# Top-k attention with a gated feed-forward layer: scores of two units ahead of the P@V of two others on TensorE

## The chip, the cores and the metric

The kernel runs on one core of one Trainium2 chip. A core has TensorE (matrix products, which write to PSUM), VectorE, ScalarE and GpSimd (elementwise work), and SyncE, whose queue issues most of the DMA transfers. Each engine runs its own instructions in the order in which they are written, and waits for the others through semaphores. The metric is the time of the whole program in device microseconds (us). Six runs of the kernel before took 1509.61 to 1519.95 us, median 1514.18.

## The reference

Attention over 8 batches of 8 heads, 576 positions, 64 elements a head, in which each query keeps only its 32 largest scores; then a feed-forward layer with g = h cos h.

```python
scores = scale * np.matmul(q, k.transpose(0, 1, 3, 2))          # (8, 8, 576, 576)
kth = np.partition(scores, -top_k, axis=-1)[..., -top_k:-top_k + 1]
scores = np.where(scores >= kth, scores, -1000000000.0)
attn = np.exp(scores - np.max(scores, axis=-1, keepdims=True))
attn = attn / (np.sum(attn, axis=-1, keepdims=True) + 1e-09)
attn_out = np.matmul(attn, v)
x = attn_out.transpose(0, 2, 1, 3).reshape(B * S, H * D)         # (4608, 512)
h = x @ w_in                                                     # w_in (512, 2048)
out = (h * np.cos(h)) @ w_out                                    # w_out (2048, 512)
```

All inputs are float32.

## The kernel before

**Units and slots.** The 4608 query rows are cut into 36 tiles of 128 rows, the 8 heads into 4 pairs. A unit is one tile of rows with one pair of heads: 144 units, in the order of the tiles. 576 is four and a half tiles, so that every ninth tile holds rows of two batches; its units have two parts, and their products are split into 64 rows each. The main loop (L778) takes one unit per slot. In slot i several units are worked on at once, each at another stage:

- u = unit i: VectorE looks for its 32nd largest scores. `topk_first` folds the 576 scores into 288 larger and 288 lesser ones (`fold`, L247, twice), reading the first half out of PSUM (`sc`) and the second out of the SBUF copy `s`; then come rounds of MAX8 and MATCH_REPLACE8 (L307, L310).
- w = unit i-1: ScalarE masks and exponentiates its scores (`bounds`, `mask`, `exponentials`, L312 to L342).
- x = unit i-2: VectorE takes the reciprocal of the sums (L346), GpSimd multiplies (L351) and splits the 32-bit words into halves (L363); SyncE's queue writes them to DRAM (`write_halves`, L368) and reads them back transposed (`transposes`, L374) into `pT`.
- z = units i-4 and i-3, in even slots only: TensorE forms P@V for both (`values`, L411, 20 matmuls a unit in program order, or 40 with two parts), and ScalarE copies the result to `xT` (`take_values`, L417).
- units i+1 and i+2, in even slots: TensorE forms their scores (`scores`, L223). By the condition at L609 the third unit of a tile with two batches is scored one slot ahead in place of two, so that the even slot before it scores one unit alone. ScalarE copies one unit's scores to `s` in each slot (`take_scores`: L233 for columns 0 to 447, L234 for the last 128).

The feed-forward layer is fed between these by `feed`, in portions: `ff1` (L468, 16 matmuls of 128x128) and `ff2` (L546, two of 128x512 in program order). The profile counts two matmul records for each float32 matmul. Copies of finished banks (L481, L556), the reduction of the angle on GpSimd (L507 to L516), the sine on ScalarE (L526) and the product on GpSimd (L533) follow.

**PSUM.** `sc` has two buffers of two banks; a unit's buffer is free when the second fold has read it, so the scores of unit i+2, formed in slot i, need the second fold of unit i in that same slot. One more tile of two banks, `rim`, holds three things: the last 128 score columns of two units (`sc_ends`), and, behind them, `room[0]`, in which P@V is built, and `room[1]`. The two banks of `mm` and `o` serve the feed-forward layer.

**Order.** The order on each engine is the order of the calls in the source; nothing reorders it. An even slot calls, for the parts that matter here: VectorE's search; `feed(1)`; `values(z)`; `scores` of units i+1 and i+2; on ScalarE `bounds` and `mask` of w, `exponentials`, `take_values(z)`, `take_scores(units[i + 1])`; then `load_weights`, `normalise`, `split`, `write_halves`, `transposes` of x, the loads of q, k and v that `at_slot` places in this slot (L188 to L204), `feed` again, twice. Slots 0 to 8 are `early_slot`, those after 140 `last_slot`; `slot` is used for 9 to 140. z is there from slot 12 on.

The buffers that bear on the order: q and k five, v six, `s` four, `pT` three, `xT` five.

Of the kernel before, what the change touches and what calls it, by code (L numbers as in the profile page):

```python
# [31 lines left out]
def kernel(  # L32
# [100 lines left out]
    def decode_second(n):  # L133

        for _ in range(min(n, len(wq["second"]))):
            st, w = wq["second"].popleft()
            wi = w.bitcast(I32)
            nc.vector.tensor_scalar(
                out=wi, in0=wi, scalar1=3, scalar2=None, op0=ALU.logical_shift_left
            )  # L140
            nc.vector.scalar_tensor_tensor(
                out=wi, in0=st[:, :, 1], scalar=-(2**31), in1=wi, op0=ALU.bitwise_and, op1=ALU.bitwise_or
            )
            wq["third"].append((st, w))
# [13 lines left out]
    units = []  # L158
# [57 lines left out]
    def scores(u):  # L216
        sc = u["sc"] = ps.tile([P, 2, 512], F32, tag="sc", name="sc", bufs=2)
        for to, k0, k1 in ((sc, 0, SB), (sc_ends[u["n"] % 2], SB, S)):
            for j in range(2):
                d = slice(j * D, (j + 1) * D)  # L220
                for b, q0, rows, r0 in u["parts"]:
                    st = pairs[b, u["hp"]]
                    nc.tensor.matmul(  # L223
                        to[r0 : r0 + rows, j, 0 : k1 - k0],
                        st["q"][d, q0 : q0 + rows],
                        st["k"][d, k0:k1],
                        start=True,
                        stop=True,
                    )

    def take_scores(u):
        s = u["s"] = work.tile([P, 2, S], F32, tag="s", name="s", bufs=4)
        nc.scalar.copy(out=s[:, :, 0:SB], in_=u["sc"][:, :, 0:SB])  # L233
        nc.scalar.copy(out=s[:, :, SB:S], in_=sc_ends[u["n"] % 2])  # L234
        if not u["folds"]:
            del u["sc"]
# [23 lines left out]
    def topk_first(u, w):  # L260

        u["top"] = tops[u["n"] % len(tops)]
        merges = [merge_first, merge_second] if w and w["folds"] else []
        if u["folds"]:
            for op in (ALU.max, ALU.min):
                fold(u, op)
                if merges:
                    merges.pop(0)(w)
        else:
            u["rest"] = work.tile([P, 2, S], F32, tag="rest", name="rest", bufs=1)  # L270
        for merge in merges:
            merge(w)
        topk_round(u, 0)

    def topk_round(u, rnd):
        top, rest, lasts = u["top"], u["rest"], TOPK // 8 - 1
        end = TOPK - 1 - 8 * rnd
        at = top[:, :, end : end - 8 if rnd < lasts else None : -1, 0]
        if u["folds"]:
            search(at, rest[:, :, 0:HS], rest[:, :, 0:HS], rnd < lasts)  # L280
            if rnd < TOPK // 16:

                low = top[:, :, 1 + 8 * rnd : 9 + 8 * rnd, 1]
                search(low, rest[:, :, HS:S], rest[:, :, HS:S], rnd < TOPK // 16 - 1)
        else:
            search(at, u["s"] if rnd == 0 else rest, rest, rnd < lasts)
        if rnd == lasts:
            del u["rest"]
# [44 lines left out]
    def exponentials(u):  # L333
        s, nd = u["s"], u.pop("nd")
        den = u["den"] = small.tile([P, 2], F32, tag="den", name="den")
        for j in range(2):
            nc.scalar.activation(  # L337
                out=s[:, j], in_=s[:, j], func=AF.Exp, bias=nd[:, j : j + 1], scale=1.0,
                accum_out=den[:, j : j + 1],
            )  # L340

        nc.scalar.activation(out=den, in_=den, func=AF.Identity, bias=eps, scale=1.0)  # L342

    def reciprocal(u):
        u["rden"] = small.tile([P, 2], F32, tag="rden", name="rden")
        nc.vector.reciprocal(u["rden"], u.pop("den"))  # L346
# [106 lines left out]
    def ff1(blk, i):  # L453
        w = blk["w"]
        nf = 256 // w
        part = i % 4
        if part == 0:
            blk["g"].append(ffw.tile([P, 1024], F32, tag="g", name="g", bufs=CHUNKS))
            ff["live"] += 1
        if part % 2 == 0:  # L460
            open_bank()
            blk["mm"] = ps.tile([P, 512], F32, tag="mm", name="mm", bufs=2)
        g, mm = blk["g"][-1], blk["mm"]
        for a in range(nf):
            f = i * nf + a
            at = (part % 2 * nf + a) * w
            for c in range(NC):
                nc.tensor.matmul(  # L468
                    mm[:, at : at + w],
                    w_in[f // FC][:, c, (f % FC) * P : (f % FC + 1) * P],  # L470
                    blk["xT"][:, c],
                    start=c == 0,
                    stop=c == NC - 1,
                )
        if part % 2 == 0:
            return
        ff["open"] -= 1
        full.append((take_first, blk, g, mm, part // 2))
# [6 lines left out]
    def take_banks():  # L485
        while full:
            take, *what = full.popleft()
            take(*what)
# [30 lines left out]
    def sines(least):  # L519

        n = sum(c[3] < ff["now"] for c in waiting)
        if n == 0 or (n < least and waiting[0][3] + 2 > ff["now"]):
            return
        for _ in range(n):
            blk, g, x, _, scale = waiting.popleft()
            nc.scalar.activation(out=x, in_=x, func=AF.Sin, bias=halfpi, scale=scale)  # L526
            sined.append((blk, g, x))
# [8 lines left out]
    def ff2(blk, i, f0):  # L536
        w = blk["w"]
        if f0 == 0:
            open_bank()
            blk["o"] = ps.tile([P, 512], F32, tag="mm", name="o2", bufs=2)  # L540
        o = blk["o"]
        per = 1024 // w
        for f in range(f0, f0 + 2):
            g = blk["g"][f // per]
            at = (f % per) * w + i * P
            nc.tensor.matmul(  # L546
                o, g[:, at : at + P], w_out[f], start=f == 0, stop=f == NF - 1
            )
        if f0 + 2 < NF:
            return  # L550
        ff["open"] -= 1
        full.append((take_second, blk, i, o))
# [27 lines left out]
    def feed(n):  # L580

        ff["tick"] += 1
        while n > 0 and ff["credit"] >= 1:
            for kind in (ff["kind"], 1 - ff["kind"]):
                if (can_first, can_second)[kind]():
                    break
            else:
                return
            if kind == 0:
                ff1(*first.popleft())  # L590
            else:
                ff2(*second.popleft())
            if kind != ff["kind"] or ff["half"]:
                ff["kind"], ff["half"] = 1 - kind, 0
            else:
                ff["half"] = 1
            n, ff["credit"] = n - 1, ff["credit"] - 1
# [18 lines left out]
    for n in range(NP, len(order)):  # L616
        i = last[order[n - 5]] if n >= 5 else 0
        at_slot.setdefault(max(i, NP + 2), []).append((load_qk, *order[n]))
        i = last_values[order[n - 6]] if n >= 6 else 0
# [53 lines left out]
    def slot(i, u, w, x, z):  # L673
        if x:
            reciprocal(x)
        if u:
            topk_first(u, w)
            decode_second(2)
        if u:
            topk_round(u, 1)  # L680
            topk_round(u, 2)
            topk_round(u, 3)
        made = scored.get(i, [])
        if z:
            take_banks()
        feed(1)
        if z:
            values(z)
        for m in made:
            scores(m)  # L690


        late = len(made) > 0

        decoding = i < EARLY + 8
        if i % 2 and not decoding:
            sines(1)
        if w:
            bounds(w)
            mask(w)  # L700
        take_banks()
        if w and late:
            exponentials(w)
        if z:
            take_values(z)
        take_scores(units[i + 1])
        if w and not late:
            exponentials(w)
        load_weights(2)
        if x:  # L710
            normalise(x)
            split(x)
            write_halves(x)
            transposes(x)

        for load, b, hp in at_slot.get(i, []):
            load(b, hp)
        gate(1)
        feed(1 if len(made) == 2 else 2)
        take_banks()  # L720
        decode_third()
        decode_first(2)
        reduce_first()
        reduce_second()
        feed(1 if len(made) == 2 else 3)
        if decoding or i == LAST:
            sines(1)
# [111 lines left out]
```

## Time and profile before

The profiled execution took 1512.73 us; its span from the first to the last instruction is 1510.9 us, at a mean granted TensorE clock of 0.963.

| engine | busy us | share of the span |
|---|---|---|
| TensorE, matmuls (PE) | 1415.1 | 94% |
| TensorE, weight loads (PEld) | 1017.4 | 67% |
| VectorE (DVE) | 1416.9 | 94% |
| ScalarE (ACT) | 1138.8 | 75% |
| GpSimd (POOL) | 1062.1 | 70% |

| group | count | busy us | mean ns of one | idle of the engine before it, us |
|---|---|---|---|---|
| L223, scores, 448 columns, on TensorE | 640 | 159.9 | 602 | 9.9 |
| L411, P@V, on TensorE | 2560 | 164.4 | 274 | 32.2 |
| L247, folds, on VectorE | 284 | 213.8 | 753 | 29.9 |
| L233, copy of 448 columns, on ScalarE | 144 | 129.4 | 899 | 3.8 |
| L417, copy of P@V, on ScalarE | 78 | 27.6 | 354 | 118.0 |

How such lines are read: "out<-in" are the names of the tiles that an instruction writes and reads; the time after the bar is the busy time of the group, then the mean of one, then how long the engine stood idle just before such instructions and, after an arrow, what ended most of that idle time. In the timeline the two numbers ahead of an engine's name are the start and the length in us, and brackets hold the idle time before. In the rows by slices each digit is the busy share of one of 40 equal slices of the span, in tenths. PEld is TensorE's loading of the stationary operand, which overlaps the matmuls; the ends of matmuls are modelled, so that one may seem to begin a little before the last has ended.

### The profile page before, as it was taken

To read this page: it belongs to the slowest core of one execution; us is meant where nothing else is said; L and a number is where in the kernel's file an instruction comes from. 1 tells how busy PE (TensorE), PEld (TensorE's weight loads), DVE (VectorE), ACT (ScalarE), POOL (GpSimd) and SP (SyncE) were. 2 spreads that over 40 slices of the span, in tenths; PEclk is the share of its full clock that TensorE was granted. 3 is DMA by queue.
4 is the path that set the end of the run, shared out by engine and by line. 5 is a ranking of instruction groups with operands and counts; after the bars stand their busy time and mean duration, and the time that the engine had idled before them with its cause. 6 is when DMAs were issued, how large, how long until landed. Compare 5 with 4: busy or idle time off the path is not lost.

```text
span 1510.9 us, 30265 instructions
## 1 busy us (share of the span) xinstructions
PE 1415.1 (94%) x10360; PEld 1017.4 (67%) x10360; DVE 1416.9 (94%) x4809; ACT 1138.8 (75%) x2294; POOL 1062.1 (70%) x806
## 2 busy tenths in 40 slices
PE   3578788999999999999999999999999999999999
PEld 2366366777677676777677776777677776777665
DVE  7999988999999999999999999999999999999831
ACT  5777666888788787888788887888778887788651
POOL 2456757777777777777777777777777777777610
PEclk6588889999999999999999999999999999999999
DMA  8343255545655456545654456555665555544300
GB/s 256 133 121 94 87 163 159 147 134 148 179 154 140 130 148 178 163 131 149 180 164 133 133 149 177 161 131 146 175 164 133 132 147 159 149 129 133 84 8 14
DMA packets 371754, 212.21 MB, mean 140 GB/s; under 512 B 321296, under 2 KB 337936, under 8 KB 371600
## 3 DMA queue, kind: packets, MB, share of 16 engines
q1 hardware_dynamic: 366192, 200.63, 47.8%
q10 hardware_dynamic: 5408, 9.65, 1.8%
q8 instruction: 81, 1.33, 0.4%
q14 instruction: 73, 0.60, 0.1%
HBM read 45.09 MB, written 87.29 MB: 88 GB/s over the span
## 4 chain that ended last, share of the span: by engine, by line
POOL 35%; DVE 23%; PE 19%; issue 12%; DMA 5%; ACT 4%; SPq 2%; POOLq 0%; ACTq 0%; DVEq 0%
POOL halves L363 10%; DVE top L307 10%; DVE rest L310 8%; POOL s L351 7%; PE o L546 7%; PE mm L468 6%; POOL g L533 6%; POOL x L516 5%; DVE rest L247 3%; PE rim L411 3%; POOL x L508 2%; POOL x L509 2%; POOL x L507 2%; DMA rows<-halves 2%; PE sc L223 2%
## 5 line engine op out<-in xcount | busy, mean ns | idle before, releaser
L307 DVE MAX8 top<-rest 128x8 f32<-128x288 f32 x1716 | 688.4, 450 | 0.0
L468 PEld LDWEIGHTS mm<-xT,w_in 128*128 128x128 f32 x4608 | 539.3, 193 | 67.6 <-issue 61.8
L546 PE MATMUL o<-w_out,g 128*128 128x512 f32 x1152 | 538.5, 601 | 6.9 <-POOL w_out L151 2.8
L468 PE MATMUL mm<-xT,w_in 128*128 128x128 f32 x4608 | 542.8, 276 | 0.8 <-ACT g L481 0.8
L310 DVE MATCH_REPLACE8 rest<-top,rest 128x288 f32<-128x288 f32 x1144 | 500.9, 446 | 0.0
L351 POOL TENSOR_SCALAR s<-s,rden 128x576 f32<-128x576 f32 x288 | 211.8, 747 | 325.8 <-DVE rden L346 322.2
L546 PEld LDWEIGHTS o<-w_out,g 128*128 128x128 f32 x1152 | 203.1, 191 | 195.6 <-issue 180.2
L363 POOL COPY halves<-s 128x2304 uint16<-128x2304 uint16 x132 | 277.5, 2102 | 13.0 <-DMA rows<-halves 4.7
L247 DVE TENSOR_TENSOR rest<-sc,s 128x576 f32<-128x576 f32 x284 | 213.8, 753 | 29.9 <-ACT s L234 22.0
L337 ACT ACTIVATE s<-s,nd 128x576 f32<-128x576 f32 x288 | 219.8, 764 | 0.8
L329 ACT ACTIVATE s<-s,nb 128x576 f32<-128x576 f32 x288 | 205.4, 760 | 0.0
L411 PE MATMUL rim<-pT,v 128*64 128x128 f32 (+1 forms) x2560 | 164.4, 274 | 32.2 <-DMA pT<-rows 24.2
L411 PEld LDWEIGHTS rim<-pT,v 128*64 128x64 f32 x2560 | 135.3, 142 | 87.2 <-issue 37.9
L223 PE MATMUL sc<-k,q 64*128 64x448 f32 (+1 forms) x640 | 159.9, 602 | 9.9 <-DMA k<-in_k_dram 9.8
L533 POOL TENSOR_TENSOR g<-g,x 128x1024 f32<-128x1024 f32 x68 | 160.7, 2363 | 9.7 <-ACT x L526 6.8
L516 POOL TENSOR_TENSOR x<-g,x 128x1024 f32<-128x1024 f32 x68 | 160.6, 2362 | 5.7
L481 ACT ACTIVATE g<-mm 128x512 f32<-128x512 f32 x144 | 84.3, 586 | 101.1 <-PE mm L468 100.1
L233 ACT COPY s<-sc 128x896 f32<-128x896 f32 x144 | 129.4, 899 | 3.8 <-PE sc L223 3.3
L417 ACT COPY xT<-rim 128x256 f32<-128x256 f32 (+1 forms) x78 | 27.6, 354 | 118.0 <-PE rim L223 102.0
L223 PEld LDWEIGHTS rim<-k,q 64*128 64x128 f32 (+1 forms) x640 | 59.7, 186 | 58.7 <-issue 56.0
L526 ACT ACTIVATE x<-x,halfpi 128x1024 f32<-128x1024 f32 x72 | 82.7, 1150 | 15.6 <-POOL x L516 8.3
L310 DVE MATCH_VALUE_LOAD rest<-top,rest 128x8 f32 x1144 | 89.4, 78 | 0.0
(52 smaller groups left out, 1159.2 us busy)
## 6 DMA issues: line engine op xcount, KB each, us to landing
rows<-halves SPq DMA_DIRECT2D x132, 576.0 KB, 2.8
out_dram<-ob ACTq DMA_DIRECT2D x36, 256.0 KB, 2.8
q<-in_q_dram SPq DMA_DIRECT2D x31, 288.0 KB, 3.7
st<-in_moe_w_in_dram SPq DMA_DIRECT2D x16, 512.0 KB, 5.9
v<-in_v_dram SPq DMA_DIRECT2D x32, 256.0 KB, 3.2
st<-in_moe_w_out_dram SPq DMA_DIRECT2D x16, 512.0 KB, 4.5
k<-in_k_dram SPq DMA_DIRECT2D x31, 144.0 KB, 3.6
k<-in_k_dram SPq DMA_DIRECT2D x32, 128.0 KB, 3.6
```

Source lines behind the costliest of these rows:

```text
L223: nc.tensor.matmul(to[r0 : r0 + rows, j, 0 : k1 - k0], st["q"][d, q0 : q0 + rows], st["k"][d, k0:k1], start=True, stop=True,)
L247: nc.vector.tensor_tensor(out=u["rest"][:, :, i * HS : (i + 1) * HS], in0=sc[:, :, 0:HS], in1=s[:, :, HS:S], op=op,)
L307: nc.vector.max(to[:, j], src[:, j])
L310: nc.vector.match_replace(rest[:, j], to[:, j], src[:, j], NEG)
L337: nc.scalar.activation(out=s[:, j], in_=s[:, j], func=AF.Exp, bias=nd[:, j : j + 1], scale=1.0, accum_out=den[:, j : j + 1],)
L351: nc.gpsimd.tensor_scalar(out=s[:, j], in0=s[:, j], scalar1=rden[:, j : j + 1], scalar2=1.0, op0=ALU.mult, op1=ALU.mult,)
L363: nc.gpsimd.tensor_copy(out=halves, in_=s.rearrange("p (k h) -> p h k", h=2))
L411: nc.tensor.matmul(o[d, to], lhsT, rhs, start=c == 0, stop=c == NT)
L468: nc.tensor.matmul(mm[:, at : at + w], w_in[f // FC][:, c, (f % FC) * P : (f % FC + 1) * P], blk["xT"][:, c], start=c == 0, stop=c == NC - 1,)
L516: nc.gpsimd.tensor_tensor(out=x, in0=g, in1=x, op=ALU.subtract)
L533: eng.tensor_tensor(out=g, in0=g, in1=x, op=ALU.mult)
L546: nc.tensor.matmul(o, g[:, at : at + P], w_out[f], start=f == 0, stop=f == NF - 1)
```

## The change

Two pairs of calls in `slot` change places. On TensorE `scores` of the units to come stands ahead of `values(z)`; on ScalarE `take_scores` stands ahead of `take_values`.

```diff
@@ -684,10 +684,10 @@
         if z:
             take_banks()
         feed(1)
+        for m in made:
+            scores(m)
         if z:
             values(z)
-        for m in made:
-            scores(m)
@@ -701,9 +701,9 @@
         take_banks()
         if w and late:
             exponentials(w)
+        take_scores(units[i + 1])
         if z:
             take_values(z)
-        take_scores(units[i + 1])
         if w and not late:
             exponentials(w)
```

No instruction is added, taken away or resized. VectorE, GpSimd and the DMA queues keep their order; on TensorE and ScalarE the blocks trade places in the 65 even slots from 12 to 140. `early_slot` and `last_slot` are left as they are.

## Prediction

> **What bounds the kernel now.** I read the page first: span, busy times, slices.
>
> ```profile
> span 1510.9 us, 30265 instructions
> PE 1415.1 (94%) x10360; PEld 1017.4 (67%) x10360; DVE 1416.9 (94%) x4809; ACT 1138.8 (75%) x2294; POOL 1062.1 (70%) x806
> ...
> PE   3578788999999999999999999999999999999999
> ...
> DVE  7999988999999999999999999999999999999831
> ```
>
> TensorE and VectorE are both full in the middle, so the question is which one sets the pace. The chain of waits gives both paces. Where it runs through TensorE, the P@V blocks start at 408.28, 426.98, 445.67, 464.36, 483.06: 18.69 us for a pair of slots. Where it runs through the work that VectorE releases, the products of L533 start at 761.32, 780.34, 799.38, 818.40, 837.43: 19.03 us. So TensorE can do a pair 0.34 us faster than VectorE. VectorE is the bound of the slots, and what costs time is VectorE standing still. From 740 to 900 us the busy times by stretch give it 159.11 of 160 us: it hardly ever does. The exceptions are in its waits, the groups and its timeline:
>
> ```profile
> DVE rest L247 <- ACT s L234: 22.0, 11, 6.6
> ```
>
> ```profile
> L247 DVE TENSOR_TENSOR rest<-sc,s 128x576 f32<-128x576 f32 x284 | 213.8, 753 | 29.9 <-ACT s L234 22.0
> ...
> L417 ACT COPY xT<-rim 128x256 f32<-128x256 f32 (+1 forms) x78 | 27.6, 354 | 118.0 <-PE rim L223 102.0
> ```
>
> ```profile
> 199.69 0.76 DVE L247 TENSOR_TENSOR rest<-sc,s 128x576 f32<-128x576 f32 x1 [4.49 <-ACT s L234]
> ...
> 262.07 0.76 DVE L247 TENSOR_TENSOR rest<-sc,s 128x576 f32<-128x576 f32 x1 [5.38 <-ACT s L234]
> ...
> 1122.45 0.76 DVE L247 TENSOR_TENSOR rest<-sc,s 128x576 f32<-128x576 f32 x1 [1.05 <-ACT s L234]
> ```
>
> The first fold of a slot waits for the copy of its scores, 22.0 us in all. One wait (6.57, the very first) and one of 0.83 at 135.54 lie before the slots that the change touches. In those slots the timeline has eight: the three shown, 2.21 at 1083.40, and 0.52, 0.28, 0.32, 0.18 at 738.62, 929.09, 1274.91, 1313.06: 14.43 us. Each follows an even slot. How it comes about at 1083.40:
>
> ```profile
> 1076.73 1.09 PE L411 MATMUL rim<-pT,v 128*64 128x128 f32 x16 [2.12 <-DMA pT<-rows]
> ...
> 1077.97 1.87 PE L223 MATMUL sc<-k,q 64*128 64x448 f32 x4
> ...
> 1081.48 0.39 PE L223 MATMUL rim<-k,q 64*128 64x128 f32 x4
> ...
> 1082.98 0.39 ACT L234 COPY s<-rim 128x256 f32<-128x256 f32 x1
> 1083.40 0.76 DVE L247 TENSOR_TENSOR rest<-sc,s 128x576 f32<-128x576 f32 x1 [2.21 <-ACT s L234]
> ```
>
> The transposed weights pT of the second unit land late, TensorE stands in the middle of P@V, the scores that VectorE needs next stand behind, and VectorE pays. An undisturbed pair:
>
> ```profile
> 826.00 1.09 PE L411 MATMUL rim<-pT,v 128*64 128x128 f32 x16
> ...
> 828.81 1.02 PE L223 MATMUL sc<-k,q 64*128 64x448 f32 x4
> ...
> 830.64 0.39 PE L223 MATMUL rim<-k,q 64*128 64x128 f32 x4
> ...
> 831.08 0.37 ACT L417 COPY xT<-rim 128x256 f32<-128x256 f32 x1 [1.27 <-PE rim L223]
> 831.35 0.91 ACT L233 COPY s<-sc 128x896 f32<-128x896 f32 x1
> 832.14 0.39 ACT L234 COPY s<-rim 128x256 f32<-128x256 f32 x1
> ...
> 833.76 0.76 DVE L247 TENSOR_TENSOR rest<-sc,s 128x576 f32<-128x576 f32 x1
> ```
>
> **Part 1, the order on TensorE.** Nothing is added or removed: in 65 even slots the 16 score matmuls go ahead of the 40 of P@V. Both together end when they did before (5.0 us here, 4.55 us when pT is there), unless one has to wait. New for the scores is that they begin 2.33 us sooner, the length of P@V. What could then hold them: (a) the release of their buffer by the second fold of the slot. At 825.03 + 0.75 = 825.78 it is done; the second unit's scores would begin at about 826.00 + 1.1, so 1.3 us are spare. Over all pairs this release comes between 1.6 us before and 0.3 us after TensorE's arrival, so at least 0.8 is spare. (b) q and k. In the four pairs after a token tile with two batches they are issued just before: k at 229.27, 577.08, 920.13, 1265.84, and with the median landing of 3.6 us they come up to 2 us after TensorE's arrival at 230.8, 579.8, 922.9, 1268.7. I take 0.3 to 1.3 us of waiting in each, some 3 us of TensorE in all, covered by its 0.34 us of room per pair (65 x 0.34 = 22 us).
>
> Where shapes change, before shows matmuls starting 0.07 us before the modelled end of the last ones at o to P@V, P@V to scores, scores to o (826.00, 828.81, 830.96), o to scores (569.99) and P@V to o (1456.67). Scores to P@V does not occur; bounds are -0.07 and, from the weight load's gap between P@V and scores, +0.17 us. I take 0; even 0.17 a pair is half of the room. The Trainium skill (TensorEngine Tiling, Key Properties) says that a change of tiling mode drains TensorE; there are three changes in a slot before and after, so its sum would be the same.
>
> **Part 2, the copies on ScalarE.** In the built program L234 now waits for the last P@V matmul, because scores' last 128 columns and P@V lie in one tile, rim; L233 waits for the scores alone. Let T be the end of the block. Before, L417, L233 and L234 follow T: s is whole at T + 1.50 (831.03 to 832.53). After, L233 runs under P@V (ScalarE sat idle 1.27 us before L417 here), L234 ends at T + 0.45, L417 at T + 0.82. So s comes 1.05 us sooner, ScalarE is through 0.7 us sooner, and xT comes 0.4 us later; its reader, L468 at 832.78, starts 1.3 us after L417, so 0.9 us remain. On VectorE this is worth nothing where the fold is not waiting (1.2 us spare at 833.76). Behind L234 stand L417 and the sine's table load; they waited for T before too. On SP, the loads of v wait for P@V, but stand behind a transposition that ends at 833.40, and those of q and k wait for scores, which are done sooner. GpSimd's work is unmoved.
>
> **Part 3, the late pT.** Scores fill the wait: a second pT may come 3.4 us after TensorE's arrival (2.2 of scores, 1.2 of the first P@V) before TensorE stands. At 1073.3 it landed at 1076.7, so P@V would end at about 1078.0, s at 1078.5; the fold wanted it at 1081.19: 2.21 saved. At 199.69: pT lands at 191.96, P@V ends at 194.37, s at 194.8, wanted at 195.20: 4.49 saved. At 262.07: P@V ends at 257.96, s at 258.4, wanted at 256.69: 1.7 remain, 3.67 saved. At 1122.45 all 1.05. The four small ones, 1.30, are within the 1.05 us that s gains. Sum: 4.49 + 3.67 + 2.21 + 1.05 + 1.30 = 12.7 us.
>
> One choice is in it: at 262.07 I let the second P@V take 2.41 us, as before, with the clock halved after a stand of 4.62. With the change the stand is 2.4 us. The rows nearest are two stands of 2.1: after 731.51 the granted clock stayed 1.00, after 1074.61 it fell (0.83 in the 6 us). Hence 2.41, or 1.38 as the first half took. The Trainium skill (TensorE: Matmul & The Clock Gate, What's actually happening) puts the fall after an idle window of 3.4 us, which 1074.61 contradicts; by it the sum would be 13.7.
>
> The profiled execution took 1512.73, its span 1510.9; the median of six is 1514.18, 1.45 above. 1512.73 - 12.7 = 1500.0; for the median, 1514.18 - 12.7 = 1501.5. VectorE's stop at 1427 is followed by 84 us of tail, which no part touches and which moves along with it.
>
> **Rivals.** A, the scores are not whole without P@V: L234 still stands behind a late pT. If the two large early waits stay in full, for their pT comes late in step with TensorE, the gain is 12.7 - 8.2 = 4.5: 1509.7. For it: at 262.07 a part stays by my own working. Against it: both ends of P@V above are rows, and scores took 2.6 to 3.8 us behind them.
> B, no change: the freed time meets another wait, TensorE's, whose own busy 20-us stretches read 20.00. It would need TensorE's 18.69 to be 19.03, so about 1514. Against it: 18.69 is what the chain shows when TensorE catches up.
> C, slower: with only two score buffers TensorE now stands at the head of each block until VectorE's second fold is done, and P@V no longer fills that. It decides once the release is 0.8 + 0.34 = 1.15 us later against TensorE than the latest row; each 0.4 us beyond costs 65 x 0.4 = 26 us: 1540. For it: without stalls TensorE runs ahead by 0.34 us a pair. Against: who is ahead loses only the lead.
>
> **Numbers.** Forecast 66%, A 18%, B 7%, C 9%. A measurement tells some 0.3% (4.5 us) from nothing: A falls half on either side of it. Faster 75%, same 16%, slower 9%. The forecast's own range is 1497 to 1506: 14.4 if every wait goes, and some 3 more for runs that waited longer than the profiled one. With A and the near side of B: 1496 to 1512.
>
> **What would show it.** VectorE's wait at L247 for L234 falls from 22.0 to about 9 us (6.57 + 0.83 + 1.7), its longest in the touched slots under 2; L417 no longer waits for L223; TensorE's stands at L411 for pT shrink to those at 184 and 251; scores start at TensorE's arrival. Wrong if L223 waits for VectorE or for k by over 20 us in all, if L247 keeps 4 or 5 us at 199 and 262, or if pairs take longer than 19.03.

## The result and the profile after

| | median us | lowest to highest | runs |
|---|---|---|---|
| before | 1515.02 | 1509.20 to 1521.79 | 46 |
| changed | 1506.62 | 1504.54 to 1509.94 | 22 |

The ratio is 0.9946, with a 95% interval of 0.9935 to 0.9957: 8.4 us faster on the medians, where 12.7 were forecast. The profiled execution of the changed kernel took 1506.67 us, at its median; that of before took 1512.73, which is 2.3 us below its median here. So the two traces show a difference of 6.0 us in the spans, and the other 2.4 us cannot be looked for in them.

The page of the changed kernel, span, busy times and slices:

```profile
span 1504.9 us, 30303 instructions
...
PE 1418.8 (94%) x10360; PEld 1020.7 (68%) x10360; DVE 1417.3 (94%) x4809; ACT 1139.8 (76%) x2294; POOL 1062.2 (71%) x806
...
PE   4587799999999999999999999999999999999999
...
DVE  8999999999999999999999999999999998999831
```

Busy times are what they were (VectorE 1417.3 against 1416.9). What has changed is standing still, and on VectorE it has not only gone but moved. Its waits (us in total, times, longest), first of the changed kernel, then the second of these rows as it was before:

```profile
DVE rden L346 <- ACT den L342: 20.8, 10, 7.0
...
DVE rest L247 <- ACT s L234: 11.4, 6, 5.6
```

```profile
DVE rden L346 <- ACT den L342: 15.0, 5, 7.0
```

And the groups of the changed kernel that answer to those shown of before:

```profile
L247 DVE TENSOR_TENSOR rest<-sc,s 128x576 f32<-128x576 f32 x284 | 213.7, 753 | 17.7 <-ACT s L234 11.4
...
L223 PE MATMUL sc<-k,q 64*128 64x448 f32 (+1 forms) x640 | 161.5, 591 | 24.1 <-DMA k<-in_k_dram 14.9
L411 PE MATMUL rim<-pT,v 128*64 128x128 f32 (+1 forms) x2560 | 164.4, 274 | 8.2 <-ACT pT L392 8.0
```

```profile
L417 ACT COPY xT<-rim 128x256 f32<-128x256 f32 (+1 forms) x78 | 28.3, 363 | 17.1 <-PE rim L411 17.1
```

Three things are read here. The idle time before the folds fell by 12.2 us (29.9 to 17.7), about what was forecast. TensorE stands before P@V fell from 32.2 to 8.2 us: of the 24.2 us that it stood for pT from the DMA, 0.2 are left, and L417 waits for P@V (17.1) and no longer for scores. But the wait at the reciprocal of L346 grew by 5.8 us (15.0 to 20.8), and TensorE's wait for k at L223 grew to 14.9; it was 9.8 before. 12.2 - 5.8 = 6.4, and the spans differ by 6.0.

By place it reads so. All the old waits in the touched slots are gone, 14.43 us in the eight that were listed (a ninth, of 0.17 at 585.96, was not). In their stead the timeline has waits at four places, all in slots next to a tile with two batches (this leaves out one wait of 0.39 us at 357.25, which before has too, at 367.07): at L247 0.42, 1.57, 0.82 and 2.13 (at 232.71, 577.22, 920.7 and 1266.8), at L346 0.71 four times and 1.31 once (at 242.82, 587.33, 930.8, 1276.92 and 1264.52). Together 9.1. Beyond the touched slots the wait at L346 in the tail is 1.6 us longer (5.28 against 3.65) and the first fold's wait at the start 1.0 shorter. -14.4 + 9.1 + 1.6 - 1.0 = -4.7. The rest of the 6.4 is the sum of small gaps before the folds, which no wait is put down to (7.5 us before, 5.9 after).

How one of the new waits comes about, in the timeline of the changed kernel:

```profile
563.90 2.50 SPq L374 DMA_TRANSPOSE pT<-rows  x1
...
566.44 0.57 SPq L188 DMA_DIRECT2D q<-in_q_dram  x1
...
568.22 0.60 SPq L191 DMA_DIRECT2D k<-in_k_dram  x1
...
569.20 0.96 PE L223 MATMUL sc<-k,q 64*64 64x448 f32 x2
...
571.59 1.08 PE L223 MATMUL sc<-k,q 64*64 64x448 f32 x5 [1.44 <-DMA k<-in_k_dram]
...
574.37 1.09 PE L411 MATMUL rim<-pT,v 128*64 128x128 f32 x16
...
576.38 0.39 PE L411 MATMUL rim<-pT,v_tail 128*64 128x128 f32 x4
...
576.82 0.37 ACT L234 COPY s<-rim 128x256 f32<-128x256 f32 x1 [2.77 <-PE rim L411]
...
577.22 0.76 DVE L247 TENSOR_TENSOR rest<-sc,s 128x576 f32<-128x576 f32 x1 [1.57 <-ACT s L234]
```

SyncE's queue is held by a transposition until 566.4, and only then issues q and k for the scores that TensorE begins at 569.20. TensorE stands for them, 1.44 us by the row of the matmuls, and the scores take 5.17 us until P@V begins at 574.37; where the loads are there it is 2.31 us (from 1261.65 in the same trace). Before, P@V stood in that place and needed neither. Everything behind is late: P@V ends at 576.8, the copy L234 after it, and VectorE waits 1.57 us for the copy. ScalarE, which stood 2.77 us at L234, then begins its next exponentials late, and in the following slot their sum comes late to L346:

```profile
587.33 0.17 DVE L346 RECIPROCAL rden<-den 128x2 f32<-128x2 f32 x1 [0.71 <-ACT den L342]
```

### The profile page after: what moved, and what is told of

It is laid out like the page before. It is cut to its first block, busy times and chain, and to the rows that moved or that the text cites. A ratio compares the mean times of both kernels' runs of the same rounds, so it can differ in the third digit from the quotient of the medians.

```text
span 1504.9 us, 30303 instructions
## 1 busy us (share of the span) xinstructions
PE 1418.8 (94%) x10360; PEld 1020.7 (68%) x10360; DVE 1417.3 (94%) x4809; ACT 1139.8 (76%) x2294; POOL 1062.2 (71%) x806
## 4 chain that ended last, share of the span: by engine, by line
POOL 33%; DVE 28%; PE 20%; issue 11%; ACT 5%; DMA 2%; SPq 1%; POOLq 0%; ACTq 0%; DVEq 0%
DVE top L307 12%; DVE rest L310 10%; POOL halves L363 9%; PE o L546 7%; PE mm L468 7%; POOL s L351 7%; POOL x L516 5%; POOL g L533 5%; DVE rest L247 4%; PE rim L411 3%; POOL x L508 2%; POOL x L509 2%; POOL x L507 2%; PE sc L223 2%; DMA k<-in_k_dram 1%
## 5 line engine op out<-in xcount | busy, mean ns | idle before, releaser
L468 PEld LDWEIGHTS mm<-xT,w_in 128*128 128x128 f32 x4608 | 540.8, 193 | 68.3 <-issue 60.7
L468 PE MATMUL mm<-xT,w_in 128*128 128x128 f32 x4608 | 544.0, 276 | 0.9 <-ACT g L481 0.8
L247 DVE TENSOR_TENSOR rest<-sc,s 128x576 f32<-128x576 f32 x284 | 213.7, 753 | 17.7 <-ACT s L234 11.4
L223 PE MATMUL sc<-k,q 64*128 64x448 f32 (+1 forms) x640 | 161.5, 591 | 24.1 <-DMA k<-in_k_dram 14.9
L533 POOL TENSOR_TENSOR g<-g,x 128x1024 f32<-128x1024 f32 x68 | 160.7, 2364 | 7.4 <-ACT x L526 7.4
L223 PEld LDWEIGHTS sc<-k,q 64*128 64x128 f32 (+1 forms) x640 | 47.7, 182 | 89.4 <-issue 21.5
L317 ACT ACTIVATE nb<-top 128x4 f32<-128x4 f32 x144 | 29.3, 203 | 95.7 <-DVE top L300 95.1
L223 PEld LDWEIGHTS rim<-k,q 64*128 64x128 f32 (+1 forms) x640 | 60.2, 184 | 56.8 <-issue 50.5
```

The source lines that it names most:

```text
L223: nc.tensor.matmul(to[r0 : r0 + rows, j, 0 : k1 - k0], st["q"][d, q0 : q0 + rows], st["k"][d, k0:k1], start=True, stop=True,)
L247: nc.vector.tensor_tensor(out=u["rest"][:, :, i * HS : (i + 1) * HS], in0=sc[:, :, 0:HS], in1=s[:, :, HS:S], op=op,)
L468: nc.tensor.matmul(mm[:, at : at + w], w_in[f // FC][:, c, (f % FC) * P : (f % FC + 1) * P], blk["xT"][:, c], start=c == 0, stop=c == NC - 1,)
L533: eng.tensor_tensor(out=g, in0=g, in1=x, op=ALU.mult)
```

## The experiments

Each group of runs (e1 to e4; e5 to e8; e9 and e10) shares one chip and its own runs of the kernel before, whose medians were 1510.51, 1511.88 and 1511.41. Ratios are to those. "Slot waits" are VectorE's waits of over 0.25 us at L247 and L346 in the slots that the change touches, without the one of some 0.4 us between 356 and 372 us that every one of these kernels has.

| run | median us | ratio (95%) | slot waits of VectorE |
|---|---|---|---|
| e1, TensorE's order alone | 1510.09 | 1.000 (0.9988 to 1.0011) | 9.2 us |
| e2, ScalarE's order alone | 1507.48 | 0.9981 (0.9964 to 0.9999) | 12.3 us |
| e3, changed, six q and k | 1498.22 | 0.992 (0.9905 to 0.9936) | none |
| e4, before, six q and k | 1509.14 | 0.9988 (0.9971 to 1.0004) | 9.4 us |
| e5, changed, again | 1506.57 | 0.9971 (0.9957 to 0.9985) | 9.4 us |
| e6, e3 with ScalarE's old order | 1499.82 | 0.9927 (0.9907 to 0.9947) | none |
| e7, changed, loads issued sooner | 1498.73 | 0.9919 (0.99 to 0.9939) | none |
| e8, before, loads issued sooner | 1542.57 | 1.0219 (1.0194 to 1.0245) | 45.4 us at L247, the start's among them |
| e9, e3's smaller buffers alone | 1506.19 | 0.9976 (0.9958 to 0.9994) | 7.6 us |
| e10, old order in four slots | 1499.64 | 0.9942 (0.9922 to 0.9963) | 1.0 us |

**e1 and e2: the two halves of the change.** In e1 `scores` stands ahead of `values` on TensorE and ScalarE keeps its order; e2 is the reverse.

```diff
e1
         feed(1)
-        if z:
-            values(z)
         for m in made:
             scores(m)
+        if z:
+            values(z)
e2
+        take_scores(units[i + 1])
         if z:
             take_values(z)
-        take_scores(units[i + 1])
```

> Scores ahead of P@V on TensorE alone; ScalarE keeps the copy of P@V ahead of the copies of scores. Theory (the gain is that scores fill TensorE's stand for late pT): VectorE's waits of 4.49, 5.38, 2.21 and 1.05 us at L247 go, s comes 1.05 us later than with both changes, which costs only the four pairs after a two-batch tile about 1 us each: 1507 to 1511 us, ratio 0.995 to 0.998. Rival (the gain is the earlier copy of the scores on ScalarE): 1515, ratio 1.000.

> Copies of scores ahead of the copy of P@V on ScalarE alone; TensorE keeps P@V first. Theory: s comes 0.37 us sooner, the late pT stands as before, L247 keeps 10 us or more of waits in the touched slots: 1513 to 1515 us, ratio 0.998 to 1.000. Rival (the gain is the copy): 1507, ratio 0.995.

The waits of e1, then of e2:

```profile
DVE rest L247 <- ACT s L234: 16.4, 7, 6.3
```

```profile
PE rim L411 <- DMA pT<-rows: 23.5, 10, 6.8
```

e2 went nearly as expected: TensorE still stands 23.5 us for pT, and the largest wait of VectorE stays (4.22 us at 257.81). Its waits at L247 in the touched slots are 8.7 us, where 10 or more were expected, and its ratio is at the low end. e1 did not go as expected in its time: a ratio of 1.000, which is what its rival named. TensorE's stands for pT fell to 1.1 us, as they should. In return VectorE waits 1.52, 1.96, 1.84 and 2.65 us at 234, 580, 924 and 1269, next to the two-batch tiles, and 1.24 at 254.78. These are 0.4 to 1.1 us longer than the changed kernel's waits at the same folds in the trace above (though e9, with the changed kernel's order, has 1.80 at 234.99); but no wait of 0.71 follows at L346, so that a two-batch tile costs about as much in both (1.96 here, 1.57 + 0.71 there, at 577). The late loads hold up both. The profiled execution of e1 is the fastest of its twelve, 2.7 us under the median, so what the other runs lost beside this its trace does not show, and that stays open. By their times, then, neither half alone has the gain, and these two runs do not tell which half carries it; e4 and e6 below do, for loads that are in time.

**e3 and e4: q and k one buffer sooner.** Six buffers let the loads of q and k be issued one pair of heads earlier; to make room, `xT` has three buffers in place of five and `ob` one in place of two. e3 is the changed kernel with this, e4 the kernel before.

```diff
-        q = st["q"] = loads.tile([P, S], F32, tag="q", name="q")
-        k = st["k"] = loads.tile([P, S], F32, tag="k", name="k")
+        q = st["q"] = loads.tile([P, S], F32, tag="q", name="q", bufs=6)
+        k = st["k"] = loads.tile([P, S], F32, tag="k", name="k", bufs=6)
...
-        i = last[order[n - 5]] if n >= 5 else 0
+        i = last[order[n - 6]] if n >= 6 else 0
```

> The changed kernel with six buffers of q and of k in place of five and their loads one pair sooner; to make room xT has three buffers in place of five and ob one in place of two. Theory (what the change gives back is TensorE standing at the head of the block for q and k in the four pairs after a two-batch tile, about 8 us of VectorE): L223's waits for q and k fall from some 27 us to under 8, VectorE's waits in the slots from 9.5 to about 1.5: 1497 to 1501 us, ratio 0.988 to 0.991. Rival (what is given back is the wait for VectorE's second fold): no different from the changed kernel, 1506 to 1507, ratio 0.9945.

> The kernel before with the same six buffers of q and k, three of xT and one of ob. Theory: before, P@V covers the late loads, so that they cost VectorE under 1 us: 1513 to 1516 us, ratio 0.998 to 1.001. Rival (the loads cost both kernels alike): about 1507, ratio 0.995.

The slot of above in e3's timeline, then two rows of its groups:

```profile
567.61 0.98 PE L223 MATMUL sc<-k,q 64*64 64x448 f32 x8
...
569.91 1.09 PE L411 MATMUL rim<-pT,v 128*64 128x128 f32 x16
...
572.37 0.37 ACT L234 COPY s<-rim 128x256 f32<-128x256 f32 x1
...
575.52 0.76 DVE L247 TENSOR_TENSOR rest<-sc,s 128x576 f32<-128x576 f32 x1
```

```profile
L247 DVE TENSOR_TENSOR rest<-sc,s 128x576 f32<-128x576 f32 x284 | 213.9, 753 | 14.1 <-ACT s L234 7.4 <-DVE rden L346 0.4
...
L223 PEld LDWEIGHTS sc<-k,q 64*128 64x128 f32 (+1 forms) x640 | 45.1, 182 | 73.4 <-DVE rest L247 24.6 <-DVE top L295 21.2 <-issue 15.1
```

The eight matmuls at the head now run in 0.98 us without a stand, P@V starts 2.30 us after the scores where it took 5.17, and the copy is there 2.8 us before VectorE's fold wants it. The ratio is a little above the 0.988 to 0.991 that were expected. All slot waits are gone (the 7.4 us at L247 lie before the touched slots), and the kernel is 8.35 us faster than the changed one in e5, though on another chip; against their own kernels before the ratios are 0.992 and 0.9971. With the old order the same buffers are worth nothing that can be told (0.9988): there P@V covers the loads. The last row shows what now releases most heads of the block: VectorE's second fold, with the small reduction L295 that runs beside it (24.6 and 21.2 us before the weight loads). Nearly all of this is 0.76 us at a time in which only the weight loads stand idle, while the product before them still runs by its modelled end; the trace of before has the same 0.76 us ahead of P@V (at 826.00), so that the sum is not time lost. The matmuls themselves stand for VectorE three times in the touched slots, 3.19 us at 164.04, 4.84 at 187.47 and 2.00 at 225.46, and this costs nothing: no wait of VectorE follows.

**e5, e6 and e9: the changed kernel again, and what else could have made e3 fast.** e6 is e3 with `take_values` ahead of `take_scores` as before; e9 is the changed kernel with the smaller `xT` and `ob` and five buffers of q and k.

```diff
e6, against e3
-        take_scores(units[i + 1])
         if z:
             take_values(z)
+        take_scores(units[i + 1])
e9, against changed
-            blk["xT"] = work.tile([P, NP, P], F32, tag="xT", name="xT", bufs=5)
+            blk["xT"] = work.tile([P, NP, P], F32, tag="xT", name="xT", bufs=3)
...
-        ob = ffw.tile([P, DM], F32, tag="ob", name="ob")
+        ob = ffw.tile([P, DM], F32, tag="ob", name="ob", bufs=1)
```

> The changed kernel once more, on the same chip as the next three. Both theories: ratio 0.993 to 0.996 to the kernel before; its profile keeps waits of some 4 to 8 us at L247 behind the four two-batch tiles and no stand of TensorE for pT beyond 1 us.

> Six buffers of q and k as in e3, scores ahead of P@V on TensorE, but ScalarE copies P@V ahead of the scores. Theory (the copies' order gains 1.05 us of slack, which is worth time only where TensorE stands for q and k): with the loads in time as fast as e3, ratio 0.990 to 0.993, no wait over 0.5 us at L247 in the touched slots. Rival (the copies' order is needed by itself, as e1 with 1.000 may be read): 0.996 to 1.000.

> The changed kernel with what e3 gave up for its room alone: three buffers of xT in place of five, one of ob in place of two; q and k keep five. Theory (the gain of e3 is the loads' sixth buffer): as the changed kernel, ratio 0.995 to 0.998, the waits behind the four two-batch tiles stay. Rival (the smaller pools are what helps): 0.991 to 0.993.

The smaller buffers do nothing by themselves (e9, 0.9976; the changed kernel, 0.9971 in e5). And with q and k in time the order of the copies is worth nothing that the intervals tell (0.9927 against 0.992, on two chips), as Part 2 had it. Set beside e4 (0.9988), e6 shows that TensorE's order carries the gain there. e5 puts the gain of the change at 5.3 us on another chip, a little below what was expected of it, against 8.4 in the result; e9's, 5.2, is the same. The changed kernel takes the same in both places (1506.57 and 1506.62); what differs is the kernel before (1511.88 and 1515.02), whose runs also spread more (12.6 us in the result, against 5.4). That pT comes more or less late from run to run would explain it, but is not shown.

**e7 and e8: loads of q and k issued ahead of the transposition, with five buffers.** In `slot` the loads go ahead of `write_halves` and `transposes` in SyncE's queue; e7 does this to the changed kernel, e8 to the kernel before.

```diff
             split(x)
+        for load, b, hp in at_slot.get(i, []):
+            if load is load_qk:
+                load(b, hp)
+        if x:
             write_halves(x)
             transposes(x)
 
         for load, b, hp in at_slot.get(i, []):
-            load(b, hp)
+            if load is not load_qk:
+                load(b, hp)
```

> The changed kernel with five buffers; in slot() the loads of q and k are issued ahead of the slot's write of the halves and its transposition, so that they start some 6 us sooner and pT comes 2 to 4 us later in the 27 slots that have such loads. Theory: L223's waits for q and k go, and the later pT is covered by the scores ahead of it: 0.990 to 0.993. Rival (pT still paces TensorE and VectorE): slower than the changed kernel, 0.997 or more.

> The kernel before with the same move of the loads. Theory (with P@V ahead, a pT that comes later by 2 to 4 us stops TensorE, then ScalarE, then VectorE): 20 or more new stands of 1 to 2 us, ratio 1.010 to 1.030. Rival (late pT was not what the change removed): 0.998 to 1.003.

SyncE's queue in e7, then the waits of e8:

```profile
560.31 0.34 SPq L188 DMA_DIRECT2D q<-in_q_dram  x1
...
561.86 0.59 SPq L191 DMA_DIRECT2D k<-in_k_dram  x1
562.56 0.54 SPq L368 DMA_DIRECT2D rows<-halves  x1
565.84 2.79 SPq L374 DMA_TRANSPOSE pT<-rows  x1
```

```profile
PE rim L411 <- DMA pT<-rows: 46.5, 21, 7.8
DVE rest L247 <- ACT s L234: 45.4, 18, 6.1
```

One edit, two signs. In this slot TensorE begins the scores at 567.57 in e7 (569.20 in the changed kernel). The loads start to leave 7.3 us before that in place of 2.8 (567.57 - 560.31 against 569.20 - 566.44); the write and the transposition stand behind them, and the transposition starts 1.7 us before the scores in place of 5.3 (565.84 and 563.90). So pT comes some 3.6 us later against the scores. The new order has the scores to fill that, and is as fast as e3 with one buffer fewer. The old order has nothing to put in TensorE's way: its stands for pT rise from 24.2 to 46.5 us, VectorE's waits from 22.0 to 45.4 us, and the kernel is some 31 us slower than before. Of stands for pT there are 21 where before had 11; 20 more, of 1 to 2 us, were expected, and some are longer (6.52 us at 239.88). This is the mechanism of the prediction at its plainest: a late pT reaches VectorE with the old order and doesn't with the new.

**e10: the old order in four slots.** The changed kernel, but in slots 18, 54, 90 and 126, whose scores find q and k late, both pairs of calls stand as before.

```diff
+        old = i % 36 == 18
+        if z and old:
+            values(z)
         for m in made:
             scores(m)
-        if z:
+        if z and not old:
             values(z)
...
+        if z and old:
+            take_values(z)
         take_scores(units[i + 1])
-        if z:
+        if z and not old:
             take_values(z)
```

> The changed kernel with the old order, on TensorE and ScalarE, in the four even slots 18, 54, 90 and 126 alone, whose scores need the pairs loaded last. Theory: the waits of 0.8 to 1.6 us at L247 near 233, 577 and 921 us and the 0.71 us at L346 one slot later shrink by more than half, those near 1264 stay, for there TensorE stood in the odd slot before: 2 to 4 us below the changed kernel, ratio 0.993 to 0.996. Rival (the loss is not in these slots): as the changed kernel, 0.997.

e10's timeline, the slot of above and, after the dots, the one wait that is left:

```profile
568.36 1.09 PE L411 MATMUL rim<-pT,v 128*64 128x128 f32 x16
...
570.69 1.28 PE L223 MATMUL sc<-k,q 64*64 64x448 f32 x8
...
574.90 0.76 DVE L247 TENSOR_TENSOR rest<-sc,s 128x576 f32<-128x576 f32 x1
```

```profile
1259.83 0.76 DVE L247 TENSOR_TENSOR rest<-sc,s 128x576 f32<-128x576 f32 x1 [1.03 <-ACT s L234]
```

With P@V first, the scores start at 570.69 and run through, and the fold doesn't wait. Four slots of 65 bring back 6.5 us against e9, the changed kernel with smaller buffers on the same chip (1506.19 to 1499.64), more than the 2 to 4 expected. The waits at the first three places are gone, 6.3 us in e9's trace. At the fourth, near 1264, little changed, as expected: the 1.03 here are at the fold that has 2.13 in the changed trace, and e9, without the old order, has 0.61 and 0.72 there and no wait of 1.31 either. What made that place dearer in the changed trace is taken up below.

So three edits that have only the late q and k in common, one more buffer, an earlier place in the queue, or P@V as cover, each take 6.5 to 8.4 us off (e3 against e5 on another chip, e7 against e5, e10 against e9), and each takes the same waits away but for e10's last. e3, e7 and e10 beat both kernels; e7 does so without another buffer.

## Why the prediction was right, and where it was wrong

**The bound and Part 3, right.** VectorE sets the pace; late pT cost it time through the scores queued behind; scores ahead of P@V take that away. The eight waits went, and L417 no longer waits for L223. The gain of this part was put too low, 14.4 in place of 12.7: at 262.07 I let 1.7 us remain, reckoning with pT landing as late as in the trace of before, followed by a slow second P@V. In the changed trace neither came: the transposition for the second unit begins 7.9 us ahead of that fold (244.54 and 252.42), where it was 5.6 us ahead of the time at which the fold was due before (251.13 and 256.69). P@V runs through from 248.55, the copy L234 begins at 251.15, and the fold doesn't wait. Why pT came sooner there is not shown, so the last 1.7 us may be luck.

**Part 1 (b), wrong, and it decides the size.** I priced the late loads of q and k in the four pairs at "0.3 to 1.3 us of waiting in each, some 3 us of TensorE in all, covered by its 0.34 us of room per pair", so nothing for VectorE. Both halves of that were off. The delay was larger. From the first score matmul to P@V a block with such loads takes 2.31 us when they are there (at 1261.65, the fourth); in the changed trace the other three took 6.20, 5.17 and 4.02 us (from 223.66, 569.20 and 913.79), 3.9, 2.9 and 1.7 us too long, 8.5 in all. The waits in brackets (2.19, 1.44 and 0.28) show less of it, since the modelled ends of the matmuls before them reach into the stand. Two figures of the working were too kind: the last of k's three transfers leaves 0.6 us after the times given (577.72 in place of 577.08 in the trace of before), and the landing took 3.9 to 4.6 us, not 3.6, in the changed trace from 563 to 580 us.

And the cover was there only in part. A room of 22 us over 65 pairs is an average; a stand at the head of one block delays the scores of that block, and VectorE has little in hand at just these folds. The trace of before says so: its small waits of 0.17, 0.28 and 0.32 at 585.96, 929.09 and 1274.91 are those of the same three folds, and I listed two of them among the gains without asking what else came late there. So the stand was paid at once, at L247, and again at L346 in the next slot through ScalarE, which stood at L234: 4.9 us of the 8.5 at these three places. With the fourth the price was 9.1 us. 14.4 - 9.1 = 5.3 us in the slots, where 12.7 was forecast; e3 and e7 give the price back in full, e10 most of it.

The other 4.2 us, near 1264, came about in another way. The block there runs in 2.31 us. But in the odd slot before it TensorE stood 1.58 us for k at 1249.46 (0.52 in the trace of before), and then ran at a granted clock of 0.50 from 1250 to 1256. In e9, with the same order, a stand of 1.50 was followed by a clock of 1.00, and its waits near 1264 are 1.3 us; in e5, where the clock fell too (0.52 and 0.50), they are 4.0. So some 2.8 of the 9.1 us go with the clock (two traces against one), which the prediction weighed only at 262.07. The four products behind the scores, first in the changed kernel, then in e9:

```profile
1252.16 3.78 PE L546 MATMUL o<-w_out,g 128*128 128x512 f32 x4
```

```profile
1253.36 1.98 PE L546 MATMUL o<-w_out,g 128*128 128x512 f32 x4
```

The rest of Part 1 held. (a) The release by the second fold delays no one: e3, where it releases the most heads, has no slot waits. The change of shape from scores to P@V, taken as nothing between -0.07 and 0.17, shows -0.07: in the timeline of the changed kernel the last scores at 574.05 are modelled to last 0.39 us, to 574.44, and P@V begins at 574.37.

**Part 2, right in its working.** L234 waits for the last P@V matmul (33.0 us of ScalarE's idle time), and e1, which leaves this out, has the longer waits at the four folds told of above; 1.05 us was worked out. xT coming 0.4 us later held no one up: TensorE's matmuls at L468 stand 0.9 us in all.

**The tail** was to move along unchanged; in this one trace it is 1.6 us longer, which the last section takes up. It comes both ways with either order (before 3.65 and e4 5.24; e3 3.65 and e7 5.29), so it is not of the order alone.

**The rivals.** A is refuted: no wait of 4 or 5 us is left at 199 and 262, L234's stand behind P@V notwithstanding. B named another wait that takes the freed time; it took 9.1 of 14.4 us, though not by TensorE's pace: undisturbed pairs still take 19.00 us (the products of L533 from 752.56 to 885.56), and TensorE has room in them. C's stand of TensorE for VectorE's fold is there, 4.43 us at 163.13 and 4.84 at 186.56 in the changed trace, but no wait of VectorE follows.

**The signs and the number.** Of what was to be seen, L417's wait and TensorE's stands for pT came as said; VectorE's wait at L247 fell to 11.4 us instead of about 9, its longest in the touched slots is 2.13, not under 2, and the scores do not start at TensorE's arrival where q and k are late. The sign of being wrong, L223 waiting "for VectorE or for k by over 20 us in all", was badly chosen. For k it is 14.9, and the harm was done, because of where it fell. For VectorE the weight loads show 47.8 us (16.7, 16.7, 10.6 and 3.8 by what ended them), so that the sign was met, and it means little: nearly all of it is the 0.76 us at a time told of at e3. The changed kernel's 1506.62 is just above the forecast's own range, 1497 to 1506, and nearer to A's 1509.7 than to the 1501.5 forecast; it is the traces that tell the two apart. That the gain comes out at 8.4 us and not nearer 5.3 is in part luck: on this chip the runs of before were slower than the profiled one, and elsewhere the gain is 5.3 (e5) and 5.2 (e9).

## What to carry to other kernels

Work that stands ahead of a producer in an in-order queue is also the cover for that producer's inputs: before moving the producer up, list what it reads that lands within the length of what it is moved past, and price each late one at the consumer, not against the average room of the engine. Room of a third of a microsecond per pair does not pay for 2 to 4 us at the one moment when the consumer has little in hand. Measure such a stand by how late the next block begins, not by the wait in brackets alone. And where two transfers share a queue, their order has the right sign only for one order of the matmuls that read them (e7 and e8: the same edit, 8 us gained on one order, 31 lost on the other), so that the two are to be tried together.

## What the runs showed of the hardware that was not expected

Whether TensorE's clock falls after a stand did not go by the length of the stand. In the changed kernel five score matmuls took 1.08 us after the stand of 1.44 at 571.59, with a granted clock of 1.00 in the 2.8 us that follow. The longest of these stands, 2.19 at 226.81, was followed by 1.00 until 229.8. After the stand of 1.58 at 1249.46 they took 1.60 us, at 0.61 until 1252:

```profile
1249.46 1.60 PE L223 MATMUL sc<-k,q 64*64 64x448 f32 x5 [1.58 <-DMA k<-in_k_dram]
```

In the tail it is the other way round. The changed kernel stands 1.74 and 1.02 us around its transpositions and then runs at 0.57 (until 1414.3); before stood 1.94 and 1.02 and kept 1.00. The 16 matmuls that follow are the first row here of the changed kernel, the second of before:

```profile
1411.15 3.24 PE L468 MATMUL mm<-xT,w_in 128*128 128x128 f32 x16
```

```profile
1418.49 1.95 PE L468 MATMUL mm<-xT,w_in 128*128 128x128 f32 x16
```

The wait of VectorE at L346 behind them is 5.28 us in the one and 3.65 in the other, and the runs of the experiments show either value, 5.24 to 5.29 (e4 to e9) or 3.64 to 3.65 (e1, e2, e3, e10). The Trainium skill (TensorE: Matmul & The Clock Gate, What's actually happening) puts the fall after an idle window of about 3.4 us; no single stand here was that long, and what decides between the two was not tried.
